# Beacon attention and a low-rank mixer on one core: v of the first batch by the hardware queues, and a written-out order for the second batch's pairs

## The chip, the core and the metric

The kernel runs on one core of a Trainium2 chip. The core has five engines that run side by side, each in the order of its own instruction stream: TensorE (PE, matrix products into PSUM), VectorE (DVE), ScalarE (ACT), GpSimd (POOL) and SyncE (SP). They wait for one another only through semaphores. Transfers run on 16 DMA engines. SP and ACT issue them on hardware queues; POOL issues them by software, and only that way converts f32 to f16 during the transfer. The metric is the device time of one execution in microseconds, as the median of the runs.

## The reference

Eight batches, 8 heads, 576 tokens, head width 64, and 16 beacon keys and values ahead of each batch's own.

```
k_all = concatenate([beacon_k, k], axis=2)
v_all = concatenate([beacon_v, v], axis=2)
scores = scale * matmul(q, k_all.T)          # causal; the beacons are seen by all
a = softmax(scores)
x = matmul(a, v_all)                         # as (batch, 576, 512)
h = x.T @ U @ V                              # rank 32, over the tokens
u = x + h.T
out = u + relu(u @ w_ch1) @ w_ch2            # 512 -> 2048 -> 512
```

Inputs and output are f32. The kernel computes in f16 with f32 sums.

## The kernel before

**Attention.** A pair is two heads, four pairs per batch, 32 in all (pair p is batch p//4, heads 2c and 2c+1 with c = p%4). For a pair, `regroup` (L217) copies q and k into token order; `qkT_units` (L223) turns both with products against the identity (L229, L231) and copies the result from PSUM on DVE (L232, L233); `score_units` (L267) has three units: two visits with products (L286) and exps on ACT (L292), and the masks on DVE (L273, L275); `av_unit` (L306), one per head, has 15 products (L310), a reciprocal and a scaling on DVE (L318, L319) into `xb`. From batch 3 on q and k are turned by DMA transposes instead (`turn_of`, L529).

**Mixer.** `mix_units` (L323) gives one `head` (20 products into `qtp`, L339, copied to `qts`) and two `part`s (L354, L364) that leave u transposed in `uT`, by two ACT and two DVE copies each. `mlp_units` (L378) serves 512 rows: 16 `g_unit`s (four products with w1, L397, and a relu on ACT L401 or DVE L403) and 16 `c_unit`s (four products with w2, L413; every fourth adds u, evicts on L426, L428 or L430, and stores).

**Order.** `manual_schedule` keeps the order in which the code emits. What belongs to the mixer waits in a list, `queue`, and `fill(n)` (L571) takes n units from it. `mix(b)` (L587) puts batch b's head and parts in, and `feed` adds the 32 units of each block of 512 rows that is ready. So a batch adds 35 units as long as it completes one block. How many are taken is written out: `FIRST` for the pairs of the first two batches, spread over a pair's units, `AHEAD` after them, `QUOTA` (4 per pair in batch 2, else 9) in the main loop, which runs the scores of pair p+1 and the transposes of p+2 beside the av of p.

**Start.** `load_first` (L474) loads q and k of batch 0 as f32: pair 0's q from ACT's queue, all else from SP's, pair by pair (`SETS`), each as a main part and a head part. `group_first` (L504) rounds them to f16 while regrouping, on ACT, DVE or POOL. Batch 0's v is loaded in two halves of four heads by POOL's queue, straight to f16 (`v_loads`, L168, six transfers a half). POOL then issues batch 1's q and k, half of its v, w1 in two halves, the casts of U and V, the other half of v, and w2 in two halves.

```python
for j in range(NT):
    a = Nb if j == 0 else 0
    nc.gpsimd.dma_start(
        out=dst[a : a + nq[j], j, :, :], in_=src[hs, ds(q0[j], nq[j]), :].rearrange("h p d -> p h d")
    )
```

`keep_warm` (L206) issues products whose result nobody reads, in the places given by `IDLE`. Tiles of tag `gT` have two buffers, shared by the first loads and the mixer's hidden layer.

Of the kernel before, what the change touches and what calls it, by code (L numbers as in the profile page):

```python
# [10 lines left out]
F32 = mybir.dt.float32  # L11
# [6 lines left out]
P = 128  # L18
# [9 lines left out]
def kernel(  # L28
# [122 lines left out]
    def emit_w2():  # L151
        w2r = moe_w_ch2.rearrange("(dc p) c -> p dc c", p=P)
        for i in range(2):
            dcs = ds(NDC // 2 * i, NDC // 2)
            nc.gpsimd.dma_start(out=w2[:, dcs, :], in_=w2r[:, dcs, :])
# [12 lines left out]
    def v_loads(src, bsrc, vs, hs):  # L168
        dst = vs[:, :].rearrange("p (c h e) -> p c h e", h=H, e=E)[:, :, hs, 0:D]
        beacon_load(nc.gpsimd, bsrc, dst[:, 0, :, :], hs)  # L170
# [5 lines that stand above are left out]
# [12 lines left out]
    def k_loads(b, L, hs):  # L188
        main_load(nc.gpsimd, k[b], L[1][0][:, hs, :], hs)
        head_load(nc.gpsimd, k[b], L[0][0][:, hs, :], hs, Nb)  # L190

    def q_loads(b, L, hs):
        main_load(nc.gpsimd, q[b], L[1][1][:, hs, :], hs)
        head_load(nc.gpsimd, q[b], L[0][1][:, hs, :], hs, 0)
# [271 lines left out]
    def load_batch(b):  # L466
        Ls[b] = qk_tiles()
        emit_loads(b, Ls[b], vss[b % 2])
# [5 lines left out]
    def load_first():  # L474

        main = gtp.tile([P, 2, H, 4 * D], F32, name="stm", tag="gT")
        head = gtp.tile([P, 2, H, D], F32, name="sth", tag="gT")
        raw["head"] = head
        hd = [loads.tile([P, H, D], F16, name=f"hd{i}", tag=f"hd{i}") for i in range(2)]
        Ls[0] = hd, [main[:, i, :, :] for i in range(2)]  # L480

        def kload(hs):
            main_load(nc.sync, k[0], main[:, 0, hs, :], hs)
            head_load(nc.sync, k[0], head[:, 0, hs, :], hs, Nb)

        def qload(eng, hs):
            main_load(eng, q[0], main[:, 1, hs, :], hs)
            head_load(eng, q[0], head[:, 1, hs, :], hs, 0)

        qload(nc.scalar, SETS[0])  # L490
        kload(SETS[0])
        beacon_load(nc.sync, beacon_k[0], head[:, 0, :, :], ALLH)

        nc.scalar.activation(out=warm, in_=ones, func=AF.Exp)
        for hs in SETS[1:]:
            kload(hs)
            qload(nc.sync, hs)

    def act_copy(out, in_):
        nc.scalar.activation(out=out, in_=in_, func=AF.Copy)  # L500
# [3 lines left out]
    def group_first(c, i, copy):  # L504

        prs.setdefault(c, []).append(regroup(Ls[0], c, i, copy))
        hs = SETS[c]
        copy(out=Ls[0][0][i][:NL, hs, :], in_=raw["head"][:NL, i, hs, :])

    def regroup_of(p):  # L510
        b, c = divmod(p, NH2)
        prs[p] = [regroup(Ls[b], c, i, nc.vector.tensor_copy) for i in range(2)]
# [9 lines left out]
    def new_qT_of(p):  # L522
        b, c = divmod(p, NH2)
        if b not in qTs:
            new_qT(b)
# [22 lines left out]
    def av_of(p):  # L548
        b, c = divmod(p, NH2)
        if c == 0:  # L550
            xbs[b] = xbp.tile([P, NT, DM], F16, name="xb", tag="xb")
        return [
            lambda i=i: av_unit(b, 2 * c + i, expts[(2 * p + i) % NE], vss[b % 2], xbs[b]) for i in range(2)
        ]


    NF = 2
    HB = 3
    AHEAD = 16
    LAG = 12  # L560
    HINT = 5

    FIRST = [0, 0, 0, 0, 10, 5, 4, 4]

    QUOTA = {2: 4}

# [34 lines left out]

    with tc.manual_schedule(engines={ENG.PE, ENG.Activation, ENG.DVE, ENG.SP, ENG.Pool}):
        load_first()
        v_loads(v[0], beacon_v[0], vss[0], HALVES[0])
        cast_small = small_loads()
        for i in range(NE):

            nc.vector.memset(expts[i][:, SLOT + gw[1] : 2 * SLOT], 0.0)
            nc.vector.memset(expts[i][:, 3 * SLOT + gw[3] : blk[(3, 4)] + P], 0.0)
        V, G = nc.vector.tensor_copy, nc.gpsimd.tensor_copy  # L610
        group_first(0, 0, act_copy)
        group_first(0, 1, V)
        keep_warm(pst([P, 512], F32, name="idle"), IDLE[0])
        t0, sc = qkT_of(0), scores_of(0)
        for u in t0:
            u()
        sc[0](IDLE[1])
        sc[1]()
        masks = sc[2]
        group_first(1, 0, G)  # L620
        group_first(1, 1, V)
        v_loads(v[0], beacon_v[0], vss[0], HALVES[1])
        for u in qkT_of(1):
            u()
        sc = scores_of(1)
        sc[0](IDLE[2])
        group_first(2, 0, G)

        Ls[1] = qk_tiles()
        group_first(3, 0, G)  # L630
        k_loads(1, Ls[1], HALVES[0])
        q_loads(1, Ls[1], HALVES[0])
        beacon_load(nc.gpsimd, beacon_k[1], Ls[1][0][0], ALLH)
        k_loads(1, Ls[1], HALVES[1])
        q_loads(1, Ls[1], HALVES[1])
        v_loads(v[1], beacon_v[1], vss[1], HALVES[0])
        emit_w1(0)
        emit_w1(1)
        cast_small()
        v_loads(v[1], beacon_v[1], vss[1], HALVES[1])  # L640
        emit_w2()

        NP1 = NF * NH2
        for p in range(NP1):
            b, c = divmod(p, NH2)
            if c == 0 and NF <= b + 1:
                load_batch(b + 1)
            seq = [masks]
            if p + 1 < NP1:
                seq.insert(0, sc[1])  # L650
                masks = sc[2]
            av, qk, sc = av_of(p), [], []
            if p + 2 < NP1:
                if p == 0:
                    seq.append(lambda: group_first(2, 1, V))
                elif p > 1:
                    seq.append(lambda p=p: regroup_of(p + 2))
                qk = [lambda i=i, p=p: qkT_of(p + 2)[i]() for i in range(2)]
            seq += av[0:1] + qk + av[1:2]
            if p + 2 < NP1:  # L660
                new_qT_of(p + 2)
                sc = scores_of(p + 2)
                if p == 0:
                    seq.append(lambda: group_first(3, 1, act_copy))
                seq.append(lambda sc=sc, p=p: sc[0](IDLE[3] if p < NH2 else 0))
            done = 0
            for i, u in enumerate(seq):
                u()
                want = FIRST[p] * (i + 1) // len(seq)
                fill(want - done)  # L670
                done = want
            if c == NH2 - 1:
                mix(b)

        fill(AHEAD)
        regroup_of(NP1)
        regroup_of(NP1 + 1)
        t0, sc, t1 = qkT_of(NP1), scores_of(NP1), qkT_of(NP1 + 1)
        for u in t0 + sc[0:1] + t1[0:1] + sc[1:3] + t1[1:2]:
            u()  # L680
            fill(1)
        for p in range(NP1, NP):
            b, c = divmod(p, NH2)
            if c == 0 and b + 1 < B:
                if b + 1 not in Ls:
                    Ls[b + 1] = qk_tiles()
                    qk_loads(b + 1, Ls[b + 1])
                v_loads(v[b + 1], beacon_v[b + 1], vss[(b + 1) % 2], ALLH)
            if c == 1 and b + 2 < B:
                Ls[b + 2] = qk_tiles()  # L690
                qk_loads(b + 2, Ls[b + 2])
            sc = scores_of(p + 1) if p + 1 < NP else []
            qk = []
            if p + 3 < NP and p + 3 >= HB * NH2:
                turn_of(p + 3)
            if p + 2 < NP:
                if p + 2 < HB * NH2:
                    regroup_of(p + 2)
                qk = qkT_of(p + 2)
            av = av_of(p)  # L700
            if c == 0 and b > NF:
                mix(b - 1)
            seq = sc[0:1] + av[0:1] + qk[0:1] + sc[1:3] + qk[1:2] + av[1:2]
            quota = QUOTA.get(b, 9)
            done = 0
            for i, u in enumerate(seq):
                u()
                want = quota * (i + 1) // len(seq)
                fill(want - done)
                done = want  # L710
        mix(B - 1)
        guard()


        queue.insert(len(queue) - 22, guard_sum)
        fill(len(queue) - 12)
        n_bad = nc.values_load(badi[0:1, 0:1], min_val=0, max_val=P)
        fill(len(queue) - HINT)
        with tc.block():
            tc.mark_branch_hint_location("general", engines=[ENG.PE, ENG.Activation, ENG.DVE, ENG.SP, ENG.Pool])  # L720
            fill(len(queue))
# [95 lines left out]
```

## Time and profile before

| | |
|---|---|
| median of 3 runs | 367.65 us (367.05 to 367.86) |
| profiled execution | 367.15 us |
| its span, first to last instruction | 365.5 us |
| PE busy | 349.8 us, 96% of the span |
| DVE, ACT, POOL busy | 204.7, 173.7, 83.9 us |
| granted PE clock, mean | 0.994 |
| DMA, mean over the span | 111 GB/s |

The profile lists groups of instructions by line, engine and tile. Busy time is the union of an engine's spans; products are pipelined, so their single durations overlap. A value in brackets with an arrow is the idle time of the engine ahead of an instruction and what ended it. The chain of waits goes back from the last instruction, at each step to whatever released it. A stage table gives the busy time of each engine in a stretch of the span. Queues of the sequencers have a q behind the engine's name (SPq).

### The profile page before, as it was taken

What the parts mean: (1) busy time and instruction counts of PE and PEld (TensorE: products, weight loads), DVE (VectorE), ACT (ScalarE), POOL (GpSimd) and SP (SyncE); (2) the same over time, 40 slices, a digit from 0 to 9 for tenths busy, and PEclk for the clock granted to TensorE, in tenths of its full rate; (3) what the DMA queues carried; (4) which work ended last, traced back from release to release, by engine and by line L of the source; (5) the groups of instructions that cost most, each with busy time, mean ns of one, the idle gap of its engine ahead of it and who ended that gap; (6) DMA issues with size and microseconds to landing.
All of it is one profiled execution on the core that took longest, in us unless ns stands there. A gap on an engine that the chain in (4) does not pass through costs nothing.

```text
span 365.5 us, 7721 instructions
## 1 busy us (share of the span) xinstructions
PE 349.8 (96%) x3040; PEld 173.5 (47%) x3040; DVE 204.7 (56%) x565; ACT 173.7 (48%) x382; POOL 83.9 (23%) x123
## 2 busy tenths in 40 slices
PE   7777999999999999999999999999999999999995
PEld 3544545545545444544445444544454555444442
DVE  4887664357776675565666666756566446223311
ACT  3976660177654553466436643674356503401300
POOL 8976436400336001800081005000000000000000
PEclk9989999999999999999999999999999999999999
DMA  9999999990999952999299917942141013013112
GB/s 178 212 151 184 194 201 156 176 170 10 145 136 163 178 80 59 121 190 137 60 111 206 131 35 101 150 74 41 63 120 26 2 57 103 14 59 87 31 44 79
DMA packets 117916, 40.52 MB, mean 111 GB/s; under 512 B 93680, under 2 KB 112112, under 8 KB 117872
## 3 DMA queue, kind: packets, MB, share of 16 engines
q0 software_dynamic: 65904, 17.54, 54.4%
q1 hardware_dynamic: 51520, 22.12, 31.0%
q8 instruction: 25, 0.41, 0.5%
q10 hardware_dynamic: 448, 0.30, 0.3%
q14 instruction: 19, 0.16, 0.1%
HBM read 37.86 MB, written 9.44 MB: 129 GB/s over the span
## 4 chain that ended last, share of the span: by engine, by line
PE 85%; DMA 6%; DVE 3%; ACT 2%; POOL 2%; issue 0%; DVEq 0%; POOLq 0%
PE cps L413 34%; PE gps L397 33%; PE po L310 6%; PE sps L286 6%; DMA w<-in_moe_w_ch_dram 2%; DMA raw<-pr 2%; PE ups L354 2%; DMA st<-in_q_dram 2%; ACT expt L292 2%; PE idle L211 1%; POOL vs L173 1%; DVE gT L403 1%; PE ups L364 1%; PE qtp L339 1%; PE tps L231 1%; DVE expt L273 1%
## 5 line engine op out<-in xcount | busy, mean ns | idle before, releaser
L292 ACT ACTIVATE expt<-sps 128x496 f16<-128x496 f32 (+2 forms) x256 | 111.1, 531 | 61.9 <-PE sps L286 61.7
L397 PE MATMUL gps<-uT,w 128*128 128x512 f16 x576 | 135.7, 379 | 1.8 <-ACT uT L374 1.2
L413 PE MATMUL cps<-w,gT 128*128 128x512 f16 x576 | 134.4, 379 | 0.0
L401 ACT ACTIVATE gT<-gps 128x512 f16<-128x512 f32 x86 | 51.8, 608 | 64.3 <-PE gps L397 62.0
L413 PEld LDWEIGHTS <-gT 128*128 128x128 f16 x576 | 52.3, 98 | 61.1 <-issue 3.7
L397 PEld LDWEIGHTS <-w 128*128 128x128 f16 x576 | 51.8, 98 | 60.8 <-issue 6.1
L403 DVE TENSOR_SCALAR gT<-gps 128x512 f16<-128x512 f32 x58 | 40.1, 691 | 45.7 <-PE gps L397 44.0
L426 DVE TENSOR_TENSOR ob<-cps,ut 128x512 f32<-128x512 f32 x32 | 22.1, 691 | 49.6 <-PE cps L413 49.1
L173 POOL DMA_DIRECT2D vs<-in_v_dram x50 | 40.8, 831 | 14.3 <-DMA st<-in_q_dram 4.9
L310 PEld LDWEIGHTS <-expt 128*128 128x128 f16 (+1 forms) x960 | 36.9, 98 | 15.0 <-DVE expt L273 2.2
L310 PE MATMUL po<-vs,expt 128*128 128x65 f16 (+1 forms) x960 | 40.3, 195 | 1.0 <-DVE expt L273 0.5
L286 PE MATMUL sps<-qT,kT 64*128 64x80 f16 (+4 forms) x384 | 33.4, 286 | 4.0 <-DVE kT L233 3.4
L319 DVE TENSOR_TENSOR xb<-po,rec 128x320 f16<-128x320 f32 x64 | 31.4, 491 | 2.2
L374 ACT ACTIVATE uT<-ups 128x240 f16<-128x240 f32 (+1 forms) x32 | 11.5, 416 | 39.3 <-PE ups L364 39.2
L273 DVE TENSOR_TENSOR expt<-expt,bigmask 128x512 f16<-128x512 f16 x64 | 26.7, 418 | 6.0 <-ACT expt L292 5.9
L163 POOL DMA_DIRECT2D vs<-in_beacon_v_dram x10 | 5.4, 538 | 100.6 <-PE po L310 100.3
L318 DVE RECIPROCAL rec<-po 128x5 f32<-128x5 f32 x64 | 12.0, 187 | 27.0 <-PE po L310 26.2
L286 PEld LDWEIGHTS <-kT 64*128 64x128 f16 x384 | 12.3, 95 | 30.1 <-issue 10.8
L372 DVE CAST uT<-ups 128x240 f16<-128x240 f32 (+1 forms) x32 | 13.1, 450 | 8.5 <-PE ups L364 8.5
L220 DVE COPY pr<-st 128x512 f16<-128x512 f16 x56 | 14.2, 296 | 1.0 <-DMA st<-in_q_dram 0.6
L260 DVE COPY qT<-raw 128x512 f16<-128x512 f16 x20 | 12.4, 619 | 2.7 <-DMA raw<-pr 2.7
L275 DVE TENSOR_TENSOR expt<-expt,mask 80x80 f16<-80x80 f16 x64 | 12.5, 196 | 0.0
(65 smaller groups left out, 157.2 us busy)
## 6 DMA issues: line engine op xcount, KB each, us to landing
out_dram<-ob SPq DMA_DIRECT2D x36, 256.0 KB, 2.3
w<-in_moe_w_ch_dram POOLq DMA_DIRECT2D x4, 1024.0 KB, 11.5
st<-in_k_dram POOLq DMA_DIRECT2D x6, 512.0 KB, 10.0
st<-in_q_dram POOLq DMA_DIRECT2D x6, 512.0 KB, 13.4
vs<-in_v_dram POOLq DMA_DIRECT2D x18, 128.0 KB, 7.5
stm<-in_k_dram SPq DMA_DIRECT2D x4, 256.0 KB, 4.6
vs<-in_v_dram POOLq DMA_DIRECT2D x12, 64.0 KB, 6.2
stm<-in_q_dram SPq DMA_DIRECT2D x3, 256.0 KB, 5.7
```

Source lines behind the costliest of these rows:

```text
L173: nc.gpsimd.dma_start(out=dst[a : a + nq[j], j, :, :], in_=src[hs, ds(q0[j], nq[j]), :].rearrange("h p d -> p h d"))
L220: copy(out=t, in_=by_token(L[1][i][:, 2 * c : 2 * c + 2, :]))
L273: nc.vector.tensor_tensor(out=e4, in0=e4, in1=bigmask, op=ALU.min)
L286: nc.tensor.matmul(ps[g, i][:, ds(o, w)], kT[hp, c, ds(P * ch, P)], qT[hp, c, ds(qa, w)], start=True, stop=True,)
L292: nc.scalar.activation(out=ex[i][:, ds(SLOT * g, gw[g])], in_=ps[g, i][:, 0 : gw[g]], func=AF.Exp, scale=scale)
L310: nc.tensor.matmul(po[:, j, :], ex[0 : nk[c], ds(blk[(c, j)], P)], vs[0 : nk[c], ds(c * H * E + h * E, E)], start=(c == 0), stop=(c == j),)
L319: nc.vector.tensor_tensor(out=xb[:, :, ds(h * D, D)], in0=po[:, :, 0:D], in1=r.broadcast_to([P, NT, D]), op=ALU.mult)
L397: nc.tensor.matmul(g[:, 0:n], w1[:, cc, ts(dc, P)], uT[:, cc, ds(t0, n)], start=(cc == 0), stop=(cc == NCC - 1))
L401: nc.scalar.activation(out=gT["t"][:, dc, 0:n], in_=g[:, 0:n], func=AF.Relu)
L403: nc.vector.tensor_scalar_max(out=gT["t"][:, dc, 0:n], in0=g[:, 0:n], scalar1=0.0)
L413: nc.tensor.matmul(ps[:m, :], gT["t"][:, dc, ds(P * i, m)], w2[:, dc, :], start=(dc == 0), stop=turned and dc == NDC - 1, skip_group_check ...
L426: nc.vector.tensor_tensor(out=ob[:m, :], in0=ps[:m, :], in1=gT["u"][:m, i, :], op=ALU.add)
```

## The change

Batch 0's v is no longer loaded and converted by POOL's queue. It comes as f32, two heads at a time, into a tile that shares a buffer with the head parts of q and k: the beacon values and pair 0's v from ACT's queue, pair 1's v from SP's queue behind pair 2's q and k, pair 2's behind pair 3's, pair 3's last. POOL rounds it to f16, pair by pair (`cast_v`), between the regroupings it already had; pair 0's k goes from ACT to POOL as well. On POOL's queue the order behind these is: half of batch 1's q and k, w1, the casts of U and V, w2, half of batch 1's v, the other half of q and k, the other half of v.

The loop over the first eight pairs now covers the first four. Pairs 4 to 7 follow a script: with the last scores of pair 5 and both masks done, 22 units of the mixer, then the av of pairs 4 and 5 with a unit behind each, two more units, then pairs 6 and 7 with regrouping, transposes and scores, and their av. `FIRST` has three numbers of that script. 36 units are asked for in place of 23.

```diff
--- before.py
+++ after.py
@@ -474,8 +474,10 @@
     def load_first():
 
         main = gtp.tile([P, 2, H, 4 * D], F32, name="stm", tag="gT")
-        head = gtp.tile([P, 2, H, D], F32, name="sth", tag="gT")
-        raw["head"] = head
+        rest = gtp.tile([P, (2 + NT) * H * D], F32, name="sth", tag="gT")
+        head = rest[:, 0 : 2 * H * D].rearrange("p (i h d) -> p i h d", h=H, d=D)
+        vst = rest[:, 2 * H * D :].rearrange("p (j h d) -> p j h d", h=H, d=D)
+        raw["head"], raw["v"] = head, vst
         hd = [loads.tile([P, H, D], F16, name=f"hd{i}", tag=f"hd{i}") for i in range(2)]
         Ls[0] = hd, [main[:, i, :, :] for i in range(2)]
 
@@ -491,10 +493,30 @@
         kload(SETS[0])
         beacon_load(nc.sync, beacon_k[0], head[:, 0, :, :], ALLH)
 
+        def vload(eng, hs):
+            eng.dma_start(
+                out=vst[Nb : Nb + nq[0], 0, hs, :], in_=v[0][hs, 0 : nq[0], :].rearrange("h p d -> p h d")
+            )
+            for j in range(1, NT):
+                eng.dma_start(
+                    out=vst[0 : nq[j], j, hs, :], in_=v[0][hs, ds(q0[j], nq[j]), :].rearrange("h p d -> p h d")
+                )
+
         nc.scalar.activation(out=warm, in_=ones, func=AF.Exp)
-        for hs in SETS[1:]:
-            kload(hs)
-            qload(nc.sync, hs)
+        beacon_load(nc.scalar, beacon_v[0], vst[:, 0, :, :], ALLH)
+        vload(nc.scalar, SETS[0])
+        for c in range(1, NH2):
+            kload(SETS[c])
+            qload(nc.sync, SETS[c])
+            if c > 1:
+                vload(nc.sync, SETS[c - 1])
+        vload(nc.sync, SETS[NH2 - 1])
+
+    def cast_v(c, copy):
+
+        dst = vss[0][:, :].rearrange("p (j h e) -> p j h e", h=H, e=E)[:, :, SETS[c], 0:D]
+        copy(out=dst[:, 0 : NT - 1], in_=raw["v"][:, 0 : NT - 1, SETS[c], :])
+        copy(out=dst[:NL, NT - 1], in_=raw["v"][:NL, NT - 1, SETS[c], :])
 
     def act_copy(out, in_):
         nc.scalar.activation(out=out, in_=in_, func=AF.Copy)
@@ -555,12 +577,13 @@
 
 
     NF = 2
+    NP1 = NF * NH2
     HB = 3
     AHEAD = 16
     LAG = 12
     HINT = 5
 
-    FIRST = [0, 0, 0, 0, 10, 5, 4, 4]
+    FIRST = [10, 9, 2]
 
     QUOTA = {2: 4}
 
@@ -601,14 +624,13 @@
 
     with tc.manual_schedule(engines={ENG.PE, ENG.Activation, ENG.DVE, ENG.SP, ENG.Pool}):
         load_first()
-        v_loads(v[0], beacon_v[0], vss[0], HALVES[0])
         cast_small = small_loads()
         for i in range(NE):
 
             nc.vector.memset(expts[i][:, SLOT + gw[1] : 2 * SLOT], 0.0)
             nc.vector.memset(expts[i][:, 3 * SLOT + gw[3] : blk[(3, 4)] + P], 0.0)
         V, G = nc.vector.tensor_copy, nc.gpsimd.tensor_copy
-        group_first(0, 0, act_copy)
+        group_first(0, 0, G)
         group_first(0, 1, V)
         keep_warm(pst([P, 512], F32, name="idle"), IDLE[0])
         t0, sc = qkT_of(0), scores_of(0)
@@ -619,58 +641,68 @@
         masks = sc[2]
         group_first(1, 0, G)
         group_first(1, 1, V)
-        v_loads(v[0], beacon_v[0], vss[0], HALVES[1])
         for u in qkT_of(1):
             u()
         sc = scores_of(1)
         sc[0](IDLE[2])
+        cast_v(0, G)
         group_first(2, 0, G)
+        cast_v(1, G)
+        group_first(3, 0, G)
 
         Ls[1] = qk_tiles()
-        group_first(3, 0, G)
         k_loads(1, Ls[1], HALVES[0])
         q_loads(1, Ls[1], HALVES[0])
         beacon_load(nc.gpsimd, beacon_k[1], Ls[1][0][0], ALLH)
-        k_loads(1, Ls[1], HALVES[1])
-        q_loads(1, Ls[1], HALVES[1])
-        v_loads(v[1], beacon_v[1], vss[1], HALVES[0])
+        cast_v(2, G)
+        cast_v(3, G)
         emit_w1(0)
         emit_w1(1)
         cast_small()
+        emit_w2()
+        v_loads(v[1], beacon_v[1], vss[1], HALVES[0])
+        k_loads(1, Ls[1], HALVES[1])
+        q_loads(1, Ls[1], HALVES[1])
         v_loads(v[1], beacon_v[1], vss[1], HALVES[1])
-        emit_w2()
-
-        NP1 = NF * NH2
-        for p in range(NP1):
-            b, c = divmod(p, NH2)
-            if c == 0 and NF <= b + 1:
-                load_batch(b + 1)
-            seq = [masks]
-            if p + 1 < NP1:
-                seq.insert(0, sc[1])
-                masks = sc[2]
-            av, qk, sc = av_of(p), [], []
-            if p + 2 < NP1:
-                if p == 0:
-                    seq.append(lambda: group_first(2, 1, V))
-                elif p > 1:
-                    seq.append(lambda p=p: regroup_of(p + 2))
-                qk = [lambda i=i, p=p: qkT_of(p + 2)[i]() for i in range(2)]
+
+        for p in range(NH2):
+            seq = [sc[1], masks]
+            masks = sc[2]
+            av = av_of(p)
+            if p == 0:
+                seq.append(lambda: group_first(2, 1, V))
+            elif p > 1:
+                seq.append(lambda p=p: regroup_of(p + 2))
+            qk = [lambda i=i, p=p: qkT_of(p + 2)[i]() for i in range(2)]
             seq += av[0:1] + qk + av[1:2]
-            if p + 2 < NP1:
-                new_qT_of(p + 2)
-                sc = scores_of(p + 2)
-                if p == 0:
-                    seq.append(lambda: group_first(3, 1, act_copy))
-                seq.append(lambda sc=sc, p=p: sc[0](IDLE[3] if p < NH2 else 0))
-            done = 0
-            for i, u in enumerate(seq):
+            if p == 0:
+                seq.append(lambda: group_first(3, 1, act_copy))
+            for u in seq:
                 u()
-                want = FIRST[p] * (i + 1) // len(seq)
-                fill(want - done)
-                done = want
-            if c == NH2 - 1:
-                mix(b)
+            sc = scores_of(p + 2)
+            sc[0](IDLE[3])
+        mix(0)
+        load_batch(2)
+
+        def run(us, n):
+            for u in us:
+                u()
+                fill(n)
+
+        run([sc[1]], 1)
+        run([masks], 2)
+        fill(FIRST[0])
+        run([sc[2]], FIRST[1])
+        run(av_of(4), 1)
+        run(av_of(5), 1)
+        fill(FIRST[2])
+        for p in (6, 7):
+            regroup_of(p)
+            run([lambda i=i: qkT_of(p)[i]() for i in range(2)], 0)
+            run(scores_of(p), 1)
+        run(av_of(6), 1)
+        run(av_of(7), 0)
+        mix(1)
 
         fill(AHEAD)
         regroup_of(NP1)
```

## The prediction

> **What bounds the kernel now.** I first asked for the busy time by stage, because a share over the whole span hides where TensorE (PE) stands still. Columns: length, then busy us and instructions of PE, its weight loads, DVE, ACT and POOL, then the granted clock, DMA share and GB/s.
>
> ```profile
> 0.00:35.00 35.00, 26.14 (x339) 15.62 (x340) 25.13 (x96) 24.63 (x58) 29.92 (x55) 0.95 1.31 180
> 35.00:74.00 39.00, 38.49 (x347) 19.85 (x348) 19.33 (x54) 14.71 (x32) 18.68 (x24) 1.00 1.78 182
> 74.00:120.00 46.00, 44.49 (x458) 22.49 (x456) 32.68 (x98) 29.51 (x66) 12.79 (x16) 1.00 1.19 126
> 120.00:300.00 180.00, 179.32 (x1581) 87.57 (x1580) 107.25 (x281) 92.06 (x203) 22.51 (x28) 1.00 0.74 97
> 361.00:365.50 4.50, 0.37 (x2) 0.00 (x0) 0.69 (x1) 0.00 (x0) 0.00 (x0) 0.93 0.18 64
> ```
>
> PE idles 8.86 us of the first 35, then 0.51, 1.51 and 0.68 up to 300 us. PE's work is the same in both kernels, so the change is worth what it does to this idle time: some of the 8.86 can be won, and nearly any new wait behind 35 us is added in full. The chain in order of time says what fills the first 35 us.
>
> ```profile
> 8.53 4.81 ACT expt L292 x11
> 13.34 0.62 POOL pr L220
> 14.19 0.70 POOL st L166
> 15.49 6.84 DMA st<-in_q_dram
> 22.61 3.55 POOL vs L173 x5
> 26.16 8.73 DMA w<-in_moe_w_ch_dram
> 34.93 1.90 PE gps L397 x8
> ```
>
> Pairs of the first batch run at ACT's and DVE's pace; then pair 4 waits for batch 1's q, then w1. Last, PE in order of time, with its idle time in brackets, and the load queues:
>
> ```profile
> 9.70 0.39 PE L231 MATMUL tps<-ident,pr 128*128 128x128 f16 x4
> 10.09 0.59 PE L211 MATMUL sps<-ident 128*128 128x512 f16 x2
> 11.41 0.88 PE L286 MATMUL sps<-qT,kT 64*128 64x496 f16 x12 [0.72 <-DVE kT L233]
> 22.65 0.21 PE L229 MATMUL tps<-ident,hd 80*128 80x80 f16 x1 [1.56 <-DMA hd<-in_q_dram]
> 52.15 0.62 PE L310 MATMUL po<-vs,expt 128*128 128x65 f16 x15 [0.26 <-DVE expt L273]
> ```
>
> ```profile
> 4.84 0.33 SPq L160 DMA_DIRECT2D sth<-in_q_dram  x1
> 7.50 0.44 SPq L166 DMA_DIRECT2D stm<-in_k_dram  x1
> SPq L160 <- DMA stm<-in_q_dram: 0.3, 1, 0.3
> SPq L131 <- DMA stm<-in_k_dram: 0.5, 1, 0.5
> SPq L132 <- DMA sth<-in_k_dram: 0.4, 1, 0.4
> ```
>
> These waits have no data behind them. Counted in program order over SP and ACT together, the issue at 4.84 is the ninth and starts when the first (q of pair 0, on ACT's queue) has landed; L131 is the eighteenth and waits for the tenth, L132 for the eleventh. So eight hardware transfers are under way at most, both queues counted as one. The reader is to keep this: a transfer put in front takes a place.
>
> The profiled execution took 367.15 us: its span 365.5 and 1.65 around it. The median of the runs, 367.65, is 0.5 above; I add the change to the median.
>
> **Part 1: v of batch 0 by hardware queues.** Removed: twelve software issues on POOL (0.66+3.96+0.52+3.66 = 8.8 us by its rows) and their traffic. Added: one beacon and 20 v issues. In program order k of pair 1 is now the 12th transfer, not the 6th, and waits for the 4th, k's head of pair 0 (issued 1.39, about 4.1 to land): start 5.5 instead of 2.82. SP issues one every 0.58 us (2.82 to 9.26 for twelve). Landing took 3.6 to 4.0 us for the first loads and 4.6 to 5.7 in the medians, with software v beside them; without that v I take 3.9, ends 3.6 and 4.8. Then:
> - q's head of pair 1 (15th): issued about 7.3, landed 11.2 instead of about 9.1. Pair 1 starts some 2 us later.
> - last v of pair 1 (24th): 12.8, landed 16.7. k's head of pair 3 (26th): 14.0, landed 17.9. q's head of pair 3 (28th): 15.2, landed 19.1; ACT's copy of it, at 15.02 before, stands ahead of pair 2's exps, so these start 3.5 to 4 us later.
> - last v of pair 3 (38th): 20.9, landed 24.8. The small loads (U, V) come behind, to about 29; only w2's issue and the mixing at 33 need them.
>
> POOL runs in order. Behind cast_v(1) (f32 copies of this size are 0.61 to 0.74 and 0.29 to 0.59 there, so 1.1) at 17.8 and group_first(3) (1.0), batch 1's first load is issued at 18.8 instead of 14.14. Its q goes out 1.35 later; it landed in 6.84 before, and the nearest rows with less beside them are 4.5 to 5.0 (20.98, 21.61). With 5.0 it is there at 25.15 instead of 22.33. PE's transposes of pair 4, at 22.65 with 1.56 idle, move by as much, and what follows to the first gps is the same work in the same order. I take **+3.0** for the front. Ends: +6 with landings of 4.8 and 6.8; and -2.4 if nothing is late, for then the 1.56 idle, the 0.58 before the first gps and a little of the slow clock go and gps starts at 32.5, the pairs' own pace of 3.8 us (8.12, 11.41, 15.54, 19.42).
>
> Pair 0's k copy goes from ACT (0.63, 0.31) to POOL (0.61, 0.29): nothing, both end with the landing of beacon_k at 5.5.
>
> **Weights.** They leave after cast_v(3), at about 26, as before (26.16), but with no v of batch 1 in front. At 211 GB/s (30 to 35 us) a half of 1.05 MB takes 5.0; with 2.5 to start, w1 is there near 33.5. gps would want it at 37.9, so it costs nothing, with 4 us of cover. The four halves end near 50 (5 to 6.5 each before), v's first half of batch 1 near 53.5; av(4) wants it at about 54. That cover is thin: 0 in the sum, up to +3.
>
> **Part 2: the script for pairs 4 to 7.** Before, filler units (0.86 of PE each) stand between the steps of these pairs. The script puts 25 units first, and few between the steps that depend on each other:
> - qkT to scores, pairs 6 and 7, no filler: last transpose to first scores 9.70+0.39 to 11.41, so 1.3 each, **2.6**.
> - pair 7's transposes wait for regroup(7), on DVE behind masks(6) and an ob copy. From pair 6's first scores: exps begin after 0.41, take 1.95+1.59, the last mask 0.60, ob 0.69, regroup 0.48: 5.7. PE has scores 0.51+0.41, three units and an identity product (2.9): 3.8. Idle **1.9**.
> - av(7) to mix(1)'s head: the queue is empty by then (35 units there, 36 asked). po at 52.15, xb done at 53.53; less 0.46 of po, **0.9**.
> - mix(1) has its 12 c units behind it, not between its parts: after the last ups two uT copies (0.92) and 0.2 of latency, **1.1**.
>
> Together 6.5; less the 0.51 that 35 to 74 us held before, **+6.0**. Ends: 4 if DVE runs ahead of the rows, 8 if PE also waits for PSUM banks.
>
> **Part 3: a shorter queue later.** A batch gives 3+32 units. By pair 7, before has used 23, the change 35; then 16, 7, and four per pair of batch 2: 62 of 70 before, 74 asked of 70 after. Pair 11 gets none of its four units (3.4 us of PE), while its successor's exps take 3.5 and PE has 1.8: about 1.0. From there on 36 are asked of 35 per batch, so the five later mixings begin on an empty queue, where 8 to 4 units stood. The head then waits for xb behind 0.5 of scores (0.9-0.5 = 0.4) and loses some cover for uT, against 0.53 that the trace shows at the first such place: 0.3 each. **+2.5**, ends 0.5 and 5.
>
> **Sum.** 3.0 + 6.0 + 2.5 = 11.5: span 377.0, and 367.65 + 11.5 = **379.2**.
>
> **The rivals.**
> - *The front is not late*: the hardware loads land quicker than issued, and only parts 2 and 3 remain. For it: 8.86 us idle, DMA freed of POOL's slow issue. Against it: the eight places and 0.58 an issue. 367.65+8.5 = 376.2, or 373.8 with the 2.4.
> - *The clock falls in the script*. After the 1.56 us idle, in a stretch where PE was busy 2.27 of 4 us (20 to 24), the granted clock was 0.88, 0.50 and 0.77 in the next three pairs of us: 1.7 us lost. Idle of 1.3, 1.9 and 1.3 within 11 us is alike; two falls give +3.4 and 382.6. Against it: 10 to 20 us had PE at 7.60 of 10 at full clock. The Trainium skill (TensorE: Matmul & The Clock Gate, Part 1) has the clock halve after at least one idle window of about 3.4 us; by that rule no wait here would do it and the sum would stay 379.2. This trace shows a fall after 1.56 at a stretch, so the row counts more.
> - *Faster*: w1 without v in front of it ends the front; gps starts at 32.5 and PE never waits in the script, because DVE and ACT, freed of filler evictions, are done first. 367.65-2.4 = 365.3. It decides once parts 2 and 3 add less than the 2.4; by the rows they add 8.5, and the two 1.3 alone reach it.
> - *No net change*: a front of -2.4 meeting just 2.4 of new waits, 367.65.
>
> **How the numbers follow.** Forecast 0.58 (own range 375 to 384), front not late 0.17, clock 0.14, faster 0.08, no change 0.03. The range 371 to 385.5 takes in the first three but for their far ends (some 0.07) and leaves out the last two. 0.2% is 0.7 us, about what a measurement of this kernel can tell from no change. Slower 0.89, same 0.03, faster 0.08.
>
> **What would show it.** Right: SP's main load of pair 1's k starting near 5.5; the first st load on POOL near 19; the first gps near 38 with no wait for w; idle of 1 to 2 us on PE ahead of sps and tps of pairs 6 and 7 (between 60 and 80 us) and again ahead of the second qtp; pair 11 without filler. Wrong: first gps before 35, or PE idle under 3 us from there to the third mixing. The sum would also be wrong if the v loads took their places in another order than program order, or if batch 1's v or k came after PE asks.

## The result, and the profile after

The changed kernel takes 384.4 us, against 367.38 for the kernel before on the same chip: a ratio of 1.045 (95% interval 1.042 to 1.048). It is slower by 17.0 us in the medians. The forecast was 379.2, range 371.0 to 385.5. One of its four runs, 389.77, was in a slower state of the chip; the median counts it, the ratio does not.

The profiled execution of the changed kernel took 383.31 us, with a span of 381.7. Its busy time by stage (same columns as ahead of the change):

```profile
0.00:35.00 35.00, 24.60 (x313) 14.79 (x314) 24.17 (x89) 21.93 (x51) 20.56 (x43) 0.95 0.86 169
60.00:80.00 20.00, 15.01 (x170) 7.87 (x169) 8.92 (x28) 7.85 (x18) 11.00 (x16) 0.91 1.85 186
120.00:140.00 20.00, 16.88 (x186) 9.37 (x186) 14.15 (x41) 12.21 (x29) 10.07 (x13) 0.83 1.76 157
140.00:300.00 160.00, 159.39 (x1432) 78.05 (x1431) 99.33 (x264) 85.09 (x192) 22.05 (x28) 1.00 0.83 101
300.00:377.00 77.00, 74.34 (x440) 34.97 (x439) 24.55 (x52) 16.51 (x32) 0.00 (x0) 1.00 0.18 53
```

Behind the front PE now stands still in three places above all: 5.0 us between 60 and 80, 3.1 between 120 and 140, 2.7 behind 300 (1.2 more lie between 80 and 100). Two of them also have a lower granted clock. PE in order of time shows the waits; in brackets is the idle time ahead of an instruction and what ended it:

```profile
36.58 13.97 PE L397 MATMUL gps<-uT,w 128*128 128x512 f16 x64 [0.53 <-ACT uT L374]
62.45 0.58 PE L286 MATMUL sps<-qT,kT 64*128 64x496 f16 x4 [1.32 <-DVE kT L233]
67.88 0.40 PE L231 MATMUL tps<-ident,pr 128*128 128x128 f16 x4 [1.38 <-DVE pr L220]
69.86 0.98 PE L286 MATMUL sps<-qT,kT 64*128 64x496 f16 x4 [1.32 <-DVE kT L233]
70.78 1.89 PE L413 MATMUL cps<-w,gT 128*128 128x512 f16 x4
79.26 0.44 PE L339 MATMUL qtp<-xb,Usb 112*32 112x128 f16 x17 [0.97 <-DVE xb L319]
125.36 0.98 PE L286 MATMUL sps<-qT,kT 64*128 64x496 f16 x4 [2.80 <-DVE kT L260]
320.67 0.28 PE L364 MATMUL ups<-Vsb,qts 32*128 32x240 f16 x4 [2.66 <-DVE qts L345]
```

The waits at 62.45, 67.88, 69.86 and 79.26 are the script's, where the forecast put them; the one at 36.58 belongs to the first mixing. The unit at 70.78 takes 1.89 us where others take 1.03: that is the clock. 125.36 is the first scores of pair 13, right behind pair 11's unfilled steps; 320.67 is the last mixing.

The 16.2 us of span can be split by points at which PE has done the same work in both traces:

| point on PE | before | after | corrected for work | cost since the point above |
|---|---|---|---|---|
| first gps | 34.93 | 36.58 | | +1.65 |
| first transposes of pair 8 | 73.94 | 93.17 | 12 units more done, 0.865 each | +7.2 |
| first gps behind the mixing of batch 2 | 119.33 | 131.33 | the 12 units even again; two av (0.46 each) and first scores (0.51) less done | +4.6 |
| first gps behind the last mixing | 305.75 | 321.84 | those three done by then | +2.7 |
| last instruction | 365.5 | 381.7 | | +0.1 |

The first two rows make no allowance for one av of 0.46 us, which the kernel before does ahead of the first gps (33.72) and the changed kernel behind it. At equal work the front costs 2.1 and the script 6.7; their sum is the same. The expectations below use 1.65 and 7.2.

So three costs were to be tested: the front 1.65, the script 7.2, the short queue 4.6 + 2.7 = 7.3.

### The profile page after: what moved, and what is told of

Its sections match the earlier page's. It is cut to its first block, busy times and chain, and to the rows that moved or that the text cites. A ratio compares the mean times of both kernels' runs of the same rounds, so it can differ in the third digit from the quotient of the medians.

```text
span 381.7 us, 7760 instructions
## 1 busy us (share of the span) xinstructions
PE 353.8 (93%) x3040; PEld 176.6 (46%) x3040; DVE 206.2 (54%) x565; ACT 172.9 (45%) x380; POOL 80.7 (21%) x121
## 4 chain that ended last, share of the span: by engine, by line
PE 81%; DVE 7%; DMA 6%; ACT 2%; POOL 1%; SPq 1%; issue 1%; ACTq 0%; POOLq 0%
PE gps L397 33%; PE cps L413 31%; PE po L310 6%; PE sps L286 6%; PE ups L354 2%; DMA hd<-in_q_dram 2%; ACT expt L292 2%; DMA raw<-pr 1%; DMA sth<-in_v_dram 1%; PE ups L364 1%; DMA sth<-in_beacon_k_dram 1%; DVE kT L233 1%; DVE qT L233 1%; DVE xb L319 1%; DMA stm<-in_k_dram 1%
## 5 line engine op out<-in xcount | busy, mean ns | idle before, releaser
L397 PE MATMUL gps<-uT,w 128*128 128x512 f16 x576 | 131.7, 379 | 1.7 <-ACT uT L374 1.1
L397 PEld LDWEIGHTS <-w 128*128 128x128 f16 x576 | 53.6, 98 | 66.1 <-issue 6.7
L286 PE MATMUL sps<-qT,kT 64*128 64x80 f16 (+4 forms) x384 | 34.3, 291 | 8.1 <-DVE kT L233 4.9
L173 POOL DMA_DIRECT2D vs<-in_v_dram x40 | 33.0, 846 | 9.4 <-DMA w<-in_moe_w_ch_dram 5.4
L163 POOL DMA_DIRECT2D vs<-in_beacon_v_dram x8 | 4.3, 543 | 97.7 <-PE po L310 97.7
L166 POOL DMA_DIRECT2D st<-in_k_dram x8 | 7.1, 884 | 32.0 <-DVE rec L318 27.2
```

Source lines behind the costliest of these rows:

```text
L173: nc.gpsimd.dma_start(out=dst[a : a + nq[j], j, :, :], in_=src[hs, ds(q0[j], nq[j]), :].rearrange("h p d -> p h d"))
L286: nc.tensor.matmul(ps[g, i][:, ds(o, w)], kT[hp, c, ds(P * ch, P)], qT[hp, c, ds(qa, w)], start=True, stop=True,)
L397: nc.tensor.matmul(g[:, 0:n], w1[:, cc, ts(dc, P)], uT[:, cc, ds(t0, n)], start=(cc == 0), stop=(cc == NCC - 1))
```

## The experiments

Ratios are to the kernel before on the same chip, with 95% intervals.

**The new loads alone.**

```diff
 load_first, cast_v: as in the changed kernel; the loop over eight pairs as before
+k_loads(1, Ls[1], HALVES[1]); q_loads(1, Ls[1], HALVES[1])
 cast_v(2, G); cast_v(3, G)
+v_loads(v[1], beacon_v[1], vss[1], HALVES[0])
 emit_w1(0); emit_w1(1); cast_small()
```

> Batch 0's v by the hardware queues and its rounding on POOL as in the changed kernel; the loop over eight pairs and the order of the weights (behind both halves of batch 1's q and k and half of its v) as before. Theory A (three separate costs: front 1.65, script 7.2, short queue 7.3): the last two are gone; but v's rounding now stands ahead of batch 1's v and of w1 on POOL, so w1 is issued near 31 instead of 26.2 and the first gps starts near 39.5 for 34.93: 367.4 + 4.6 = 372.0. Rival B (the new loads are what costs, all along the kernel, and the script is paid for by them): 380 or more. Rival C (w1 is not in the way, only pair 4 is late): 369.0.

Measured: 1.018 (1.014 to 1.023), 373.8 us; span 371.2, or 5.7 over before. The first gps:

```profile
38.41 2.98 PE L397 MATMUL gps<-uT,w 128*128 128x512 f16 x8 [3.28 <-DMA w<-in_moe_w_ch_dram]
```

The line, from PE in order of time, has w1 in the way, as theory A said: the first gps is 3.5 us late. The 3.28 us of waiting is followed by a slow clock (eight products in 2.98 us; 1.90 before), which adds 1.7 of the remaining 2.2. Rivals B and C are out. The run also shows why the change puts the weights first: with v rounded on POOL they come late otherwise.

**v by software again, script kept.**

```diff
 load_first()
+v_loads(v[0], beacon_v[0], vss[0], HALVES[0])
-group_first(0, 0, G)
+group_first(0, 0, act_copy)
 ...
+v_loads(v[0], beacon_v[0], vss[0], HALVES[1])
 ...
-cast_v(0, G) ... cast_v(3, G)
```

> The changed kernel with its first part undone: batch 0's v by POOL's queue as before, no rounding on POOL, pair 0's k on ACT. Script and weights' order stay. Theory A: only the front's 1.65 goes, 382.7 (382 to 383.2), first gps near 34.9. The forecast's own front term of 3.0 would give 381.4. Rival B (the loads carry the cost): 375 or less.

Measured: 1.046 (1.042 to 1.051), 384.1 us. Its time can't be told from that of the change, so it shows only that the loads don't carry the cost; the front's own cost rests on traces. In this one the first gps starts at 34.64, that is 1.94 earlier than with the change, as theory A has it; but 1.9 us are lost again behind the last mixing, where the clock fell in this execution and not in that of the changed kernel. Its script has the same waits (1.32, 1.38, 1.33, 0.97). First the stages of the changed kernel, then those of this one, two us each:

```profile
66.00:68.00 2.00, 0.62 (x9) 0.39 (x7) 1.64 (x6) 0.26 (x2) 0.62 (x1) 1.00 1.93 176
68.00:70.00 2.00, 0.68 (x11) 0.49 (x11) 1.49 (x4) 0.00 (x0) 1.01 (x2) 0.97 3.11 142
70.00:72.00 2.00, 2.00 (x7) 0.43 (x4) 0.00 (x0) 1.51 (x4) 2.00 (x3) 0.50 3.02 183
72.00:74.00 2.00, 2.00 (x14) 0.70 (x13) 0.00 (x0) 1.17 (x5) 1.43 (x3) 0.67 1.63 196
```

```profile
64.00:66.00 2.00, 0.62 (x8) 0.35 (x7) 1.71 (x7) 0.32 (x2) 0.02 (x1) 1.00 0.44 31
66.00:68.00 2.00, 0.67 (x11) 0.50 (x13) 1.49 (x4) 0.00 (x0) 2.00 (x3) 1.00 0.61 139
68.00:70.00 2.00, 2.00 (x17) 0.71 (x18) 0.00 (x0) 1.65 (x4) 1.65 (x3) 1.00 1.14 134
```

PE is busy 1.30 and 1.29 of 4 us in both; in one the clock falls to 0.50, in the other it stays at 1.00. From the first gps to that of the second mixing the one takes 81.95-36.58 = 45.4 us, the other 78.48-34.64 = 43.8: this fall cost 1.5.

**Twelve units more left in the queue.**

```diff
-    AHEAD = 16
+    AHEAD = 4
```

> The changed kernel with AHEAD 4 in place of 16: twelve units more stay in the queue, 39 used by pair 8 as before the change. Theory A (the short queue costs 4.6 around pair 11 and 2.7 at the last mixing): both go, 384.4 - 7.3 = 377.1, no wait over 1 us on PE behind 100 us. Rival D (the wait at pair 11 is that of late DMA transposes, whatever the queue holds): stays within 1 us of 384.4. The forecast's 2.5 for this term: 381.9.

Measured: 1.021 (1.016 to 1.027), 375.2 us; about 9 us of the 17 are gone. Behind 100 us the longest wait on PE is 1.04, and the last mixing has none. The span, 374.1, is 7.6 shorter. Its first gps came 0.7 later (37.24), and its clock stayed at 1.00 in the script, worth the 1.5 of the paragraph above: 7.6 + 0.7 - 1.5 = 6.8 are left for the short queue, against 7.3. Rival D is out.

Up to the end of the script this kernel is the changed one, instruction for instruction. Its waits there were the same (1.32, 1.37, 1.32, 0.97), and its DMA share around the third of them was higher (3.56 and 3.90 from 68 to 72 us, for 3.11 and 3.02), yet its clock did not fall. So the fall can stay away with these loads and under this traffic; what decides is open.

**The short queue alone, in the kernel before.**

```diff
-    AHEAD = 16
+    AHEAD = 28
```

> The kernel before with AHEAD 28 in place of 16: the shorter queue alone, without the new loads and without the script. Theory A (the short queue costs 4.6 around pair 11 and 2.7 at the last mixing whatever stands ahead of it): 367.4 + 7.3 = 374.7, with a wait near 2.8 us on PE at pair 11 and one near 2.7 at the last mixing. Rival I (it only costs that together with the script's delay): 368 or less.

Measured: 1.029 (1.023 to 1.033), 377.3 us; its profiled span is 374.9, or 9.4 over before. On PE in order of time the two waits of the changed kernel are there, of the same length:

```profile
116.46 0.98 PE L286 MATMUL sps<-qT,kT 64*128 64x496 f16 x4 [2.80 <-DVE kT L260]
312.44 0.28 PE L364 MATMUL ups<-Vsb,qts 32*128 32x240 f16 x4 [2.67 <-DVE qts L345]
```

Here the clock fell behind both (0.88 from 100 to 120, 0.91 from 300 to 320), behind the last mixing as well, which accounts for most of the difference between 9.4 and 7.3: from the wait's end to the last instruction it takes 62.5 us here and 61.0 in the changed kernel. Nothing of the loads or of the script is in this kernel: the largest of the three costs comes from taking twelve units too early. Rival I is out.

**The check of the sums behind the last mixing.** Why 2.7 there, where other mixings on an empty queue lose nothing? DVE in the changed kernel:

```profile
319.74 0.49 DVE L452 TENSOR_REDUCE allg<-good 128x1 f32<-128x320 f32 x1
320.26 0.16 DVE L453 TENSOR_SCALAR bad<-allg 128x1 f16<-128x1 f32 x1
320.33 0.28 DVE L345 CAST qts<-qtp 128x128 f16<-128x128 f32 x1
```

`guard()` is emitted ahead of the units that are left, so `qts` stands behind its nine instructions (317.81 to 320.42).

```diff
 mix(B - 1)
+fill(4)
 guard()
```

> The changed kernel with four units (the last head, both parts and one g unit) ahead of the range check of the sums, which DVE does before the last mixing. Theory F: with the queue empty the 2.66 us wait at the last mixing is qts standing behind that check on DVE; it goes: 384.4 - 2.7 = 381.7, up to 1.5 more where the clock fell behind it. Rival G (qts waits for PE's or xb's own latency, as at the other mixings): no change, 384.4.

Measured: 1.038 (1.032 to 1.044), 382.9 us. The wait is gone: from the last head to the first gps behind it 2.2 us (320.19 to 322.42) for 4.9 (316.99 to 321.84). Theory F holds by the trace. The medians can't show it: the four runs took 379.62 to 384.03, the longer ones at the lower mean clock (0.991 and 0.987 in the two shorter, 0.976 and 0.972 in the two longer). In the profiled one the clock fell once more, at 36 us, and twice as long in the script, so that its span, 382.3, is even above the changed kernel's.

**Idle products in the script.**

```diff
+if p == 7: keep_warm(pst([P, 512], F32, name="idle"), 6)
 run([lambda i=i: qkT_of(p)[i]() for i in range(2)], 0)
-run(scores_of(p), 1)
+sc = scores_of(p); run([lambda: sc[0](6)] + sc[1:], 1)
```

> The changed kernel with six products whose result nobody reads (1.3 us) in each of the three waits of pairs 6 and 7: ahead of both first scores and ahead of pair 7's transposes. No work moves. If the clock that fell to 0.50 at 70 to 72 us costs 1.7 us (rival of the forecast, seen in the trace of after): it stays at 1.00 there and the time is 382.7. If the fall costs nothing, because DVE and ACT set the pace there: 384.4 to 384.8.

Measured: 1.044 (1.039 to 1.049), 383.1 us. The clock stays at 1.00 from 60 to 78. The script takes 80.17-35.54 = 44.6 us, 0.8 more than the 43.8 without fall and 0.7 less than with one: the products overstay the waits by some 0.3 each. So by the traces the fall is real and cost 1.5 in the changed kernel, and idle products buy back half. The ratio, 1.044, can't be told from the change's 1.045.

**Units between transposes and scores** (with AHEAD 4).

```diff
-FIRST = [10, 9, 2]
+FIRST = [8, 7, 2]
-    run([lambda i=i: qkT_of(p)[i]() for i in range(2)], 0)
+    run([lambda i=i: qkT_of(p)[i]() for i in range(2)], 1)
```

> The kernel with AHEAD 4 (375.2 measured), and a mixer unit behind each transposing unit of pairs 6 and 7; FIRST 8, 7, 2, so that the same 36 are asked in all. Theory A: PE waits there for DVE's copies alone, so both 1.32 us waits ahead of the first scores go: 375.2 - 2.6 = 372.6. Rival E (DVE and ACT set the pace of pairs 6 and 7, a unit put in between only moves the wait to the next step): within 1 us of 375.2.

Measured: 1.024 (1.019 to 1.029), 376.3 us: no gain. Both waits of 1.32 are gone in its trace, and from the first transposes of pair 6 to the first gps of the second mixing it takes 21.3 us with four units (3.5) and one addition of u (0.2) more than the 20.0 us of the kernel with AHEAD 4: 2.4 less. But in this execution the front ended early, and the script ran into its own data, as PE in order of time shows:

```profile
34.01 11.18 PE L397 MATMUL gps<-uT,w 128*128 128x512 f16 x51 [0.59 <-DMA w<-in_moe_w_ch_dram]
50.45 1.51 PE L310 MATMUL po<-vs,expt 128*128 128x65 f16 x15 [3.31 <-DMA vs<-in_v_dram]
```

v of batch 1 stands behind all four halves of the weights; it was there at 50.45, and in the run with idle products it still held PE up by 0.23 at 52.59. In this execution the 3.31 and a fall of the clock behind it (0.86 from 35 to 60) ate the gain. Theory A holds locally. Rival E's time came in, but not by its cause: the waits left over in the script, 1.27 and 0.97, are no longer than without the units.

**Three attempts to beat both.** The first sends batch 1's first q and k at 7 us, SP's part of batch 0's v behind all of q and k, w1 ahead of batch 1's v, with the loop of before.

> An attempt on both kernels: batch 0's v by the hardware queues, but behind all of q and k; batch 1's first q and k issued by POOL at about 7 us instead of 14 to 16; w1 ahead of batch 1's v; the loop over eight pairs, FIRST and weights behind half of batch 1's v otherwise as in the kernel before. Theory A (the front ends with pair 4's data and pair 3's q; what follows is a full PE): pair 4 waits no longer, the clock stays up at 24 us, first gps near 33, 367.0 - 1.8 = 365.2. Rival H (eight places and the DMA engines are the limit: what is issued early only delays pairs 1 to 3 or their v): 367 to 370.

Measured: 1.028 (1.024 to 1.032), 377.6 us, worse than rival H. PE's longest wait at pair 4 is 0.48, but PE waits for v's rounding at 14.3 and 19.9 (1.3 and 1.4), for the rounding of U and V at the mixing (3.3 in all), whose loads now come last on SP, and the clock is at 0.80 from 35 to 60. The first gps comes at 42.74, where 33 was expected. The trace of before has none of these waits.

The second moves batch 1's first five loads ahead of one rounding in the kernel before:

```diff
+k_loads(1, Ls[1], HALVES[0]); q_loads(1, Ls[1], HALVES[0]); beacon_load(...)
 group_first(3, 0, G)
-k_loads(1, Ls[1], HALVES[0]); q_loads(1, Ls[1], HALVES[0]); beacon_load(...)
```

> The kernel before, with batch 1's first five loads (half of k and q, beacon_k) one step earlier on POOL, ahead of the rounding of pair 3's k (0.9 us). Nothing of the change is in it. If the front ends with pair 4's q (1.56 us of wait at 22.65) and the clock falls because of that wait: the wait shrinks to some 0.7, the clock stays up, 367.4 - 1.5 = 365.9. If pair 3, whose k is rounded 3.3 us later, is late instead (asked for at 17.05): 367.4 to 369.

Measured: 0.9986 (0.9956 to 1.0017): no difference that can be told. In the trace the wait of pair 4 falls from 1.56 to 0.47, the clock stays at 1.00 at 24 us and the span is 0.8 shorter.

The third adds AHEAD 8 to it:

> An attempt on both kernels: the kernel before with batch 1's first five loads one step earlier (364.7 us of span against 365.5 in its profile) and AHEAD 8, so that 16 units instead of 8 stand behind batch 2. Theory A (a longer queue covers what a shorter one bared): the waits of 0.53 and 0.67 ahead of the first gps of the mixings of batches 2 and 3 go, 366.9 - 0.8 - 1.2 = 364.9. Rival J (those two waits are uT's own latency, and eight units are cover enough): 366 to 367. If the eight units taken from the pairs ahead are missed there: above 367.5.

Measured: 1.006 (1.003 to 1.010), slower by little, though clear of 1. The waits at the mixings do go, and another comes earlier. The stage from 140 to 300 us:

```profile
140.00:300.00 160.00, 160.00 (x1435) 78.33 (x1435) 95.55 (x252) 79.10 (x176) 21.00 (x26) 1.00 0.72 95
```

PE in order of time at pair 10:

```profile
95.59 0.58 PE L286 MATMUL sps<-qT,kT 64*128 64x496 f16 x4 [2.44 <-DVE kT L260]
```

The wait goes back to the transposing DMAs that begin with batch 3: DVE stood 3.48 us, until one issued at 86.69 had landed at 92.95. Twelve units fewer in hand cost 9.4 us of span in the kernel before. Eight more cost 0.8 in the profiled executions (365.5 for 364.7), and more by the ratios (1.006 for 0.999). No version here beats the kernel before by a measurable amount.

## Why the prediction was right in sign, and where it was wrong

**The front: +3.0 forecast, +1.65 in the profile, 2.1 at equal work.** The step that failed is the counting of places "in program order over SP and ACT together". The changed kernel in order of time, one line each of SP's queue, ACT's queue, POOL and ACT:

```profile
2.82 0.43 SPq L166 DMA_DIRECT2D stm<-in_k_dram  x1
4.14 0.32 ACTq L497 DMA_DIRECT2D sth<-in_v_dram  x1
15.61 0.89 POOL L166 DMA_DIRECT2D st<-in_k_dram  x1
17.14 0.63 ACT L522 ACTIVATE pr<-stm 128x512 f16<-128x512 f32 x1 [2.15 <-DMA stm<-in_q_dram]
```

k of pair 1 starts at 2.82 as before, not at 5.5; ACT's first v transfer is the one that waits, until 4.14. It is the ninth by time of issue, and pair 0's first transfers land then. So eight places there are, but given out in the order of issue in time. The trace of before could not tell the two orders apart, since there they were the same. With pairs 1 and 2 on time, what is left of the step is right: pair 3's q holds ACT up (2.15 us; 17.14 for a forecast of 19.1) and batch 1's first load goes at 15.61 (forecast 18.8). That the transposes of pair 4 still start at 25.17, as forecast (25.15), is luck: batch 1's last q piece was issued 2.3 earlier than forecast (17.84 for 20.15) and took 2.3 longer to land (7.29 for 5.0). And the front is one execution's: in the five profiled with these loads and this order the first gps came between 34.0 and 37.2, for 34.93 before.

**The weights: nothing forecast, nothing found**, issued at 26.56. The thin cover that was named (v of batch 1 for av(4)) held in the profile after, and broke by 3.31 us where the front was shorter.

**The script: +6.0 forecast, 6.7 found at equal work.** Its waits were 1.32 twice (forecast 1.3 each), 1.38 (1.9), 0.97 (0.9) and 0.53 (1.1): 5.5 for a forecast of 6.5, or 5.0 when the 0.51 of before is taken off. The rest is the clock, 1.5, which the sum put at nothing and which stood among the rivals at 0.14, with two falls where one came. That the term came near is thus in part luck: its waits were 1.0 too long and the fall was missing. The fall is a matter of the execution: with the same instructions and waits the clock stayed at 1.00 in the run with AHEAD 4 and fell in the changed kernel and in the run with `guard()` later, there for twice as long. The Trainium skill (TensorE: Matmul & The Clock Gate, Part 1) calls the activity window free-running and says that the number of matmuls a kernel runs at the low clock at its start therefore varies from run to run. The executions of equal waits agree with that for falls later on. It also asks for about 3.4 us of idle; here single waits of 1.3 to 1.4 with PE busy 1.30 of 4 us were followed by a fall, so the measurement decides against that part.

**The short queue: +2.5 forecast, 7.3 found.** This is the term that was mis-sized most. The count was right (pair 11 got no unit, later mixings met an empty queue). Its price was not: pair 11 was costed at 1.0 by the exps alone. Some lines of the chain of waits there show what stands one behind the other once no unit is left:

```profile
113.67 4.69 DMA raw<-pr
118.38 0.61 DVE qT L260
122.23 2.01 ACT expt L292 x5
124.27 0.43 DVE expt L273
124.80 0.51 DVE kT L260
125.36 0.97 PE sps L286 x3
```

Pair 13's kT is copied on DVE behind masks that wait for pair 12's exps: 0.32 + 2.80 of idle, then 2.5 more by the clock at 0.50 (5.97 us from 125.36 to the first gps for work that takes 3.5 at full clock), less about 1.0 that before idled at these steps: 4.6. The 2.5 isn't the clock's alone: where the clock came back sooner, in the run with `guard()` later, PE stood 1.16 us for uT at this place instead. And of the five mixings, costed at 0.3 each, four cost nothing and the last 2.7, because `guard()` had been hidden by units that are gone. The prediction never named that check as something the queue covers.

**The sum** 11.5 was short of the span's 16.2 by 4.7: front 0.9 too much, script 0.7 too little, short queue 4.8 too little. The time, 384.4, lies inside the range of 371 to 385.5 but above the 375 to 384 given to the main forecast. The direction was right for the reason given: the script and the shorter queue add waits to a PE that had almost none to win back.

## What to carry to other kernels

When one engine is busy nearly all the time, a stock of independent work is what hides the dependent steps. Moving units forward is not free even where they fill real idle time: ask which later steps lived on that stock, and cost the first step that meets an empty queue by its whole chain, not by its slowest link. Count a list of fillers to its end, as far as the last use, and look there for work that was emitted ahead of it and had always been hidden.

## What the runs showed of the hardware

- The granted clock fell to 0.50 behind waits of 1.3 to 3.3 us, in some executions and not in others with the same waits (in the script to 0.50 in two, 1.00 in two). Once, at 36 us of the run with `guard()` later, it fell with no single wait above 0.6 us in the 5 us ahead. Worked out from the clock of two-us stages, all 21 falls of the twelve traces behind 6 us and ahead of the last 10 us lasted 3.4 us, or twice or three times that. A fall cost 1.5 us in the script, 2.8 when it lasted twice as long, and up to 2.5 at pair 11, where it came in all five traces with an empty queue.
- The eight places for hardware transfers, one set for both queues, go by the time of issue as far as these rows show: ACT's queue stood still until 4.14 while SP's went on at 2.82 and 3.29.
